# Strassen products for two more token pairs of K in layer two, later reloads, and four weight sums in front of an eviction

## The chip, the cores and the metric

The kernel runs on one core of a Trainium2 chip. A core has five engines, each with a queue of its own that it works off in order: TensorE (PE; its weight loads, PEld, overlap its matmuls), VectorE (DVE), ScalarE (ACT), GpSimd (POOL) and SyncE (SP), which here only issues DMAs. Matmuls write to PSUM, eight banks of 128 x 512 f32; everything else is in one large SBUF tensor, "arena". Engines wait for each other on semaphores. The metric is device time in microseconds, the median of several runs.

## The reference

Two blocks, A and B, are applied twice in turn to x, 2048 tokens of 1024 channels: A, B, A, B. "Layer one" is the first A and B, "layer two" the second.

```python
def _A_ref(x, wqkv, wo):               # H = 32 heads of Dh = 32
    q, k, v = split(x @ wqkv)
    phi = lambda t: jnp.where(t > 0, t + 1, jnp.exp(t)) + 1e-6
    pq, pk = phi(q), phi(k)
    kv = jnp.einsum("bhsd,bhse->bhde", pk, v)
    z = jnp.einsum("bhsd->bhd", pk)
    num = jnp.einsum("bhqd,bhde->bhqe", pq, kv)
    den = jnp.einsum("bhqd,bhd->bhq", pq, z)[..., None] + 1e-6
    return (num / den) @ wo
def _B_ref(x, w_gate, w_up, w_down):   # F = 3584
    return ((x @ w_gate) * (x @ w_up)) @ w_down
x = x + _A_ref(_layernorm(x), wqkv, wo)
x = x + _B_ref(_layernorm(x), w_gate, w_up, w_down)
```

(`split` stands for the reshape into q, k and v by heads.)

## The kernel before

**Strassen products.** Large products are cut into 2 x 2 blocks and done with seven block products instead of eight (one level), those of block B in part with a second level inside. The sums of operand blocks that this needs are made by VectorE (`tt`, line 849). The joins of partial results are VectorE additions from PSUM to PSUM with a copy that ScalarE made before.

**Order.** The program writes every engine's queue by hand. Each instruction goes in with the bytes and banks that it reads and writes, and the waits follow from that. So the order in which the Python code calls its steps is the order of every queue, SP's among them.

**K and Q of block A.** The 16 token tiles of 128 are taken as 8 pairs. K of a pair is either plain (line 979: four steps of eight 128x512 matmuls, two tiles by two halves of the columns, 32 in all) or by one Strassen level (line 1175: seven steps of four matmuls, 28 in all). In layer two all of Q (pairs 0 to 6 here) is by Strassen; K is plain for pairs below `KP0` and by Strassen from there on. The seven steps, in their order, use four PSUM banks A, B, C, D:

- step 0 multiplies into A, and ScalarE copies A to B (line 1187 for K, 1185 for Q);
- step 1 uses the sum s1, into C, and ScalarE copies C away (1191);
- step 2 uses s2, into B, and VectorE joins B and the copy into D (1179);
- step 3 finishes A;
- step 4 uses s3, into B, and a join into C follows (1179);
- step 5 uses s4 and finishes D;
- step 6 finishes B, which it must not touch before the join of step 4 has read it.

A finished bank goes through an exponential on ScalarE (1077, 1073) and on VectorE through a minimum (658 for K, 656 for Q; not where the exponential came with a bias) and an eviction (1104, or 1093 for two banks at once in plain pairs). GpSimd adds K to its running sum (1014).

A table of tokens, `KQ_SEQ`, sets the order of these steps. `K21` is step 1 of K of pair 2, `Q05` step 5 of Q of pair 0. `S20` to `S23` are the token sums s1 to s4 for pairs 2 and 3 together (line 849, 128x2x512), which K and Q share; `S40` and `S60` do the same for the pairs from 4 and 6. `L` moves the layer norm on by a step (ScalarE 474 and 494 for the statistics of a token tile, GpSimd 476, 496 and 498, VectorE 508, then a store to `xn_scratch` and a DMA transpose). `X` reloads one tile of normalized tokens from `xn_scratch`, `V`, `W` and `O` load weights. The last steps of a pair (its evictions) are issued one step of the table later.

**The end of block A's first stage.** The product of K and the normalized tokens (line 1409) comes next. Its first matmul needs all 16 reloaded tiles.

**Block B, the down pass.** Seven products, named by digits; the last, "3", is in layer one's first pass by a second level (`two_level`, lines 2044 to 2070): seven steps 1, 5, 6, 7, 2, 3, 4 for two parts p, with ScalarE copies (2048, 2062), VectorE joins (2051) and evictions (`evict`, 852). Between its steps the next pass is begun: `pro` is a list of that pass's first steps, and `pro_step(pro, 1)` calls them until one has put a matmul in. Among them are four weight sums (849, `sums`) that the next pass's first second-level product (1676) needs.

Of the kernel before, what the change touches and what calls it, by code (L numbers as in the profile page):

```python
# [180 lines left out]
def build_kernel(nc, A_x, A_wqkv, A_wo, B_w_gate, B_w_up, B_w_down, out):  # L181
# [14 lines left out]
    KSTR = True  # L196
    NEB = 3
    KQ_SEQ = {True: "L S30 Q20 S31 T L K30 S32 K31 L K32 Q21 S33 L Q22 K33 T S40 Q23 Q30 K40 K41 S41 L K42 Q31 Q32 Q33 L S42 K43 L Q34 K50 L Q35 Q36 S50 S43 K51 L Q40 L S51 S52 K52 Q41 Q42 Q43 L K53 Q44 Q45 L K60 Q46 K61 S60 Q50 S53 K62 Q51 S61 Q52 S62 Q53 Q54 K63 Q55 Q56 K70 Q60 K71 Q61 S63 Q62 L K72 Q63 Q64 Q65 K73 Q66 V",
              False: "K00 S00 S01 K01 S02 S03 L K02 K03 K10 L X K11 Q00 K12 Q01 X L Q02 K13 Q03 Q04 K20 X S20 Q05 S21 K21 S22 L Q06 S23 Q10 K22 X Q11 Q12 K23 Q13 L K30 X Q14 S40 Q15 S41 K31 S42 Q16 S43 Q20 X L K32 Q21 Q22 K33 Q23 X K40 Q24 L K41 Q25 K42 Q26 X K43 Q30 K44 K45 L Q31 K46 X Q32 Q33 K50 Q34 S60 K51 Q35 S61 L X S62 K52 S63 Q36 K53 Q40 K54 Q41 X K55 Q42 L K56 Q43 K60 Q44 K61 X Q45 K62 Q46 K63 L Q50 K64 X Q51 K65 Q52 K66 Q53 K70 L X Q54 K71 Q55 K72 Q56 K73 X Q60 K74 L Q61 K75 Q62 K76 Q63 X Q64 L Q65 Q66 V W O"}
    L1P0 = 3  # L200
    L1QS = 3
    QLAG = 0.409
# [3 lines left out]
    SPOS = 0.867  # L206
    SSTEP = 0.063
    CUP = 9
    KP0 = 4

    L2SETS = {(False, 0): "15", (False, 1): "15", (True, 0): "1532", (True, 1): "1532"}
    ORDERS = {
# [78 lines left out]
    P = _Prog(V_PT + 64)  # L291
# [42 lines left out]
    with ExitStack() as es:  # L334
# [1230 lines left out]
        def layer_B(lnp, nxt, first):  # L1565
# [322 lines left out]
            def down(ps_, ticks, tail, pro=()):  # L1888
# [26 lines left out]
                l2j = "3" if first and ps_ == 0 else ""  # L1915
# [90 lines left out]
                def two_level(q):  # L2006
# [47 lines left out]
                    for si, i in enumerate((1, 5, 6, 7, 2, 3, 4)):  # L2054
                        for p in range(2):
                            hi, lo = dst[p], dst[p + 2]
                            if i == 1:
                                mm(1, p, tmp[p], 0, True)
                                seed(p, hi)
                            elif i == 5:  # L2060
                                mm(5, p, tmp[p], 1, False)
                                P.add("act", (lambda p: lambda e: e.copy(c5[p][0], psb(tmp[p])[:, 256:512]))(p), prd=[tmp[p]], wr=c5[p][1])
                            elif i == 6:
                                mm(6, p, tmp[p], 0, False)
                                join(p, hi)
                            elif i == 2:
                                mm(2, p, hi, 0, False)
                            elif i == 3:
                                mm(3, p, hi, 1, False)
                                evict(p, hi)  # L2070
                            elif i == 7:
                                mm(7, p, tmp[p], 0, False)
                                seed(p, lo)
                                join(p, lo)
                            else:
                                mm(4, p, lo, 0, False)
                                evict(p + 2, lo)
                            if q == "3" and i in (3, 4):
                                pro_step(pro, 1)
                        if q != "3" and i in (1, 5, 7, 2):  # L2080
                            ex_pop(2 if l2j else 1)
                        if l2j and i == 1:
                            SQ.pop(0)()
                        if i in ((1, 3) if l2j else (5, 7, 3, 4)):
                            ring_issue()
                        if i in (5, 7, 3, 4):
                            ticks(q, {5: 0, 7: 1, 3: 2, 4: 3}[i])
# [26 lines left out]
                for qi, q in enumerate(DPROD[first, ps_]):  # L2114
# [13 lines left out]
                    for hf in range(2):  # L2128
                        n = n_of[q, str(hf)]
# [241 lines left out]
```

## Time and profile before

| | |
|---|---|
| median of 3 runs | 1433.35 us (1432.63 to 1433.55) |
| the profiled execution: time, span | 1432.78 us, 1431.0 us |
| instructions on TensorE, VectorE, ScalarE, GpSimd | 8430, 2024, 1540, 309 |
| K and Q stage of layer two | about 730.6 to 824.8 us of the span |
| end of layer one's first down pass | about 475.8 to 489.6 us |

In the rows that follow, times are us from the start of the span, and a row of the timeline has start, duration, engine, line, operation, output and inputs, and a count where equal instructions were merged. What stands in brackets is the engine's idle time ahead of it and what ended it. A row of groups has busy time and the mean duration in ns. SPq is SP's issuing of DMAs. A matmul of 512 columns shows 379 ns from its start to its end, though the next begins after 216.

### The profile page before, as it was taken

What the parts mean: (1) busy time and instruction counts of PE and PEld (TensorE: products, weight loads), DVE (VectorE), ACT (ScalarE), POOL (GpSimd) and SP (SyncE); (2) the same over time, 40 slices, a digit from 0 to 9 for tenths busy, and PEclk for the clock granted to TensorE, in tenths of its full rate; (3) what the DMA queues carried; (4) which work ended last, traced back from release to release, by engine and by line L of the source; (5) the groups of instructions that cost most, each with busy time, mean ns of one, the idle gap of its engine ahead of it and who ended that gap; (6) DMA issues with size and microseconds to landing.
All of it is one profiled execution on the core that took longest, in us unless ns stands there. A gap on an engine that the chain in (4) does not pass through costs nothing.

```text
span 1431.0 us, 22547 instructions
## 1 busy us (share of the span) xinstructions
PE 1421.5 (99%) x8430; PEld 813.3 (57%) x8430; DVE 1166.9 (82%) x2024; ACT 733.2 (51%) x1540; POOL 296.8 (21%) x309
## 2 busy tenths in 40 slices
PE   9999999999999999999999999999999999999999
PEld 4444444555544655554764444456666477666658
DVE  7878887889878799878878878779877877777886
ACT  4752367777720255552256523667776116777521
POOL 5644632000000000003334346301000400000160
PEclk9999999999999999999999999999999999999999
DMA  7316867987977999985798167589986689788657
GB/s 235 106 28 183 182 136 196 284 294 251 318 284 246 332 303 290 299 258 199 274 338 210 35 176 171 131 226 271 284 260 199 226 305 309 251 263 261 211 192 254
DMA packets 362541, 331.73 MB, mean 232 GB/s; under 512 B 178496, under 2 KB 305472, under 8 KB 361920
## 3 DMA queue, kind: packets, MB, share of 16 engines
q1 hardware_dynamic: 362432, 330.29, 76.9%
q8 instruction: 66, 1.08, 0.3%
q14 instruction: 43, 0.35, 0.1%
HBM read 239.27 MB, written 67.37 MB: 214 GB/s over the span
## 4 chain that ended last, share of the span: by engine, by line
PE 93%; DVE 3%; ACT 1%; DMA 1%; issue 1%; SPq 1%; POOL 1%; DVEq 0%; ACTq 0%
PE ps L1601 25%; PE ps L1676 17%; PE ps L2139 14%; PE ps L2044 9%; PE ps L1507 8%; PE ps L1409 8%; PE ps L1175 6%; PE ps L979 4%; PE ps L989 2%; DVE arena L849 1%; DMA arena<-in_B_w_down_dram 1%; PE ps L1421 1%; ACT arena L494 0%; DMA arena<-in_A_x_dram 0%; SPq L442 0%
## 5 line engine op out<-in xcount | busy, mean ns | idle before, releaser
L849 DVE TENSOR_TENSOR arena<-arena 128x512 f16<-128x512 f16 (+9 forms) x784 | 476.7, 636 | 73.0 <-ACT arena L1720 45.1
L1601 PE MATMUL ps<-arena 128*128 128x512 f16 x1808 | 446.8, 379 | 0.6 <-ACT ps L1631 0.6
L1676 PE MATMUL ps<-arena 128*128 128x256 f16 x2324 | 312.2, 273 | 2.1 <-DVE arena L849 0.9
L852 DVE SCALAR_TENSOR_TENSOR arena<-ps,arena 128x512 f16<-128x512 f32 (+2 forms) x396 | 263.0, 685 | 43.8 <-PE ps L2139 17.9
L1676 PEld LDWEIGHTS ps<-arena 128*128 128x128 f16 (+1 forms) x2324 | 226.1, 98 | 105.1 <-DVE ps L1695 4.7
L1601 PEld LDWEIGHTS ps<-arena 128*128 128x128 f16 (+1 forms) x1808 | 176.6, 98 | 141.7 <-ACT ps L1631 1.1
L2139 PE MATMUL ps<-arena 128*128 128x512 f16 (+1 forms) x896 | 194.2, 379 | 0.0
L1606 ACT ACTIVATE arena<-ps 128x512 f16<-128x512 f32 x224 | 134.1, 598 | 91.7 <-PE ps L1601 89.7
L2092 POOL TENSOR_TENSOR arena<-arena 128x512 f32<-128x512 f32 x44 | 69.8, 1596 | 424.5 <-ACT arena L2090 339.5
L2139 PEld LDWEIGHTS ps<-arena 128*128 128x128 f16 x896 | 87.7, 98 | 105.7
L2044 PE MATMUL ps<-arena 128*128 128x256 f16 (+1 forms) x1176 | 130.3, 273 | 0.1
L2044 PEld LDWEIGHTS ps<-arena 128*128 128x128 f16 x1176 | 114.5, 98 | 15.2 <-DVE ps L2051 0.4
L1695 DVE TENSOR_TENSOR ps<-ps,arena 128x256 f32<-128x256 f32 x220 | 92.3, 428 | 31.9 <-PE ps L1676 16.3
L1409 PE MATMUL ps<-arena 128*128 128x512 bf16 x512 | 115.4, 379 | 0.0
L485 POOL TENSOR_SCALAR arena<-arena 128x1 f32<-128x1 f32 x43 | 16.4, 382 | 472.5 <-DVE arena L484 472.5
L1507 PE MATMUL ps<-arena 128*128 128x512 bf16 x512 | 111.5, 379 | 0.0
L1692 ACT COPY ps<-ps 128x256 f32<-128x256 f32 x220 | 81.1, 368 | 51.4 <-PE ps L1676 43.8
L1175 PE MATMUL ps<-arena 128*128 128x512 bf16 (+1 forms) x420 | 95.1, 379 | 0.4 <-DVE ps L1179 0.3
L1315 POOL TENSOR_TENSOR arena<-arena 128x1024 f16<-128x1024 f32 x32 | 79.8, 2494 | 69.6 <-DVE arena L1313 61.7
L1631 ACT COPY ps<-ps 128x512 f32<-128x512 f32 x112 | 64.2, 573 | 49.2 <-PE ps L1676 43.5
L1014 POOL TENSOR_TENSOR arena<-arena 128x512 f32<-128x512 f32 x60 | 73.6, 1245 | 69.4 <-DVE arena L1104 33.6
L1507 PEld LDWEIGHTS ps<-arena 128*128 128x128 f16 x512 | 50.1, 98 | 59.8
(81 smaller groups left out, 1275.8 us busy)
## 6 DMA issues: line engine op xcount, KB each, us to landing
arena<-w_scratch SPq DMA_DIRECT2D x84, 512.0 KB, 5.1
arena<-sp_scratch SPq DMA_DIRECT2D x56, 512.0 KB, 5.8
arena<-t_scratch SPq DMA_DIRECT2D x27, 896.0 KB, 5.9
arena<-in_B_w_down_dram SPq DMA_DIRECT2D x18, 896.0 KB, 7.0
w_scratch<-arena SPq DMA_DIRECT2D x28, 512.0 KB, 5.9
sp_scratch<-arena SPq DMA_DIRECT2D x28, 512.0 KB, 4.1
arena<-in_B_w_gate_dram SPq DMA_DIRECT2D x42, 256.0 KB, 5.2
arena<-in_B_w_up_dram SPq DMA_DIRECT2D x42, 256.0 KB, 3.6
```

What stands on the lines that cost most here:

```text
L849: P.add("dve", lambda e: e.tensor_tensor(out=out, in0=a, in1=b, op=op), rd=rd, wr=wr, prd=prd)
L852: P.add("dve", lambda e: e.scalar_tensor_tensor(out=out, in0=a, scalar=sc, in1=b, op0=ALU.mult, op1=op1), rd=rd, wr=wr, prd=prd)
L1175: P.add("pe", lambda e: [e.matmul(psb(bank), x[:, k, :], w[:, k, :], start=(start and k == 0), stop=(k == 3), skip_group_check=True) for k ...
L1409: return [e.matmul(psb(bank), xr[:, t, j * 128:(j + 1) * 128], pk[:, h, t, :], start=(t == 0), stop=(t == NST - 1)) for t in range(NST)]
L1507: return [e.matmul(psb(bank), xnT[:, g, i * 128:(i + 1) * 128], wp[:, g, dh * 512:(dh + 1) * 512], start=(dh == 0 and g == 0), stop=(g == ...
L1601: P.add("pe", lambda e: [e.matmul(psb(bank), w[:, k, :], x[:, k, :], start=(start and k == 0), stop=(k == 3), skip_group_check=True) for k ...
L1606: P.add("act", lambda e: e.activation(t, psb(bank), AF.Copy, scale=SG), prd=[bank], wr=r)
L1676: P.add("pe", lambda e: [e.matmul(psb(bank)[:, 256 * half:256 * half + 256], w[:, k, :], xx[:, k, :], start=(start and k == 0), stop=(k == ...
L1692: P.add("act", lambda e: e.copy(psb(dst[c])[:, 0:256], lo), prd=[bk], pwr=[dst[c]])
L1695: P.add("dve", lambda e: e.tensor_tensor(out=psb(dst[c])[:, 256:512], in0=lo, in1=c5, op=ALU.add), prd=[bk], rd=rc5, pwr=[dst[c]])
L2044: P.add("pe", lambda e: [e.matmul(psb(bank)[:, 256 * half:256 * half + 256], a[:, k, :], w[:, k, :], start=(start and k == 0), stop=(k == ...
L2139: return [e.matmul(psb(bank), hv[:, 7 * hf + k, t * 128:(t + 1) * 128], w[:, k, :], start=(start and hf == 0 and k == 0), stop=(hf == 1 an ...
```

## The change

`KP0` goes from 4 to 2: K of pairs 2 and 3 of layer two is by Strassen too, so six pairs in all. The table's order for layer two is new; among other things the first reload of normalized tokens comes after K of pair 3 instead of early in pair 1. And in `two_level`, in layer one's first pass, the next pass's steps are called behind step 2 of the second part until one has put a VectorE instruction in.

```diff
-              False: "K00 S00 S01 K01 S02 S03 L K02 K03 K10 L X K11 Q00 K12 Q01 X L Q02 K13 Q03 Q04 K20 X S20 Q05 S21 K21 S22 L Q06 S23 Q10 K22 X Q11 Q12 K23 Q13 L K30 X Q14 S40 Q15 S41 K31 S42 Q16 S43 Q20 X L K32 Q21 Q22 K33 Q23 X K40 Q24 L K41 Q25 K42 Q26 X K43 Q30 K44 K45 L Q31 K46 X Q32 Q33 K50 Q34 S60 K51 Q35 S61 L X S62 K52 S63 Q36 K53 Q40 K54 Q41 X K55 Q42 L K56 Q43 K60 Q44 K61 X Q45 K62 Q46 K63 L Q50 K64 X Q51 K65 Q52 K66 Q53 K70 L X Q54 K71 Q55 K72 Q56 K73 X Q60 K74 L Q61 K75 Q62 K76 Q63 X Q64 L Q65 Q66 V W O"}
+              False: "K00 S00 S01 K01 S02 S03 L K02 K03 K10 L K11 Q00 K12 Q01 L Q02 K13 Q03 Q04 K20 S20 Q05 S21 K21 S22 L Q06 S23 K22 Q10 K23 Q11 K24 L K25 Q12 K26 Q13 K30 Q14 K31 L Q15 K32 Q16 S40 K33 S41 Q20 S42 K34 L S43 K35 Q21 K36 X Q22 Q23 K40 Q24 L K41 Q25 X K42 Q26 K43 Q30 K44 L X K45 Q31 K46 Q32 X Q33 K50 Q34 L S60 K51 Q35 S61 X K52 Q36 S62 K53 Q40 S63 L K54 X K55 Q41 K56 Q42 X Q43 K60 Q44 L K61 Q45 X K62 Q46 K63 X Q50 K64 X K65 Q51 X K66 Q52 X Q53 K70 L Q54 X K71 Q55 K72 X Q56 K73 X Q60 K74 L X K75 Q61 K76 Q62 Q63 Q64 Q65 Q66 V W O"}
...
-    KP0 = 4
+    KP0 = 2
...
                             elif i == 2:
                                 mm(2, p, hi, 0, False)
+                                if l2j and p:
+                                    n = len(P.streams["dve"])
+                                    while len(P.streams["dve"]) == n:
+                                        pro.pop(0)()
```

TensorE, where K of pair 2 begins, before: Q04, K20 in plain form (L979), Q05 (it waits for a weight block, d_qb3), K21, and Q06 (d_ptq3 is another). A name s_... is an engine's semaphore, d_... that of a DMA.

```order
L1175 MATMUL ps<-arena 128x512 [waits s_dve]
L1175 MATMUL ps<-arena 128x512 x3
L979 MATMUL ps<-arena 128x512 x8
L1175 MATMUL ps<-arena 128x512 [waits d_qb3]
L1175 MATMUL ps<-arena 128x512 x3
L979 MATMUL ps<-arena 128x512 x8
L1175 MATMUL ps<-arena 128x512 [waits d_ptq3,s_dve]
L1175 MATMUL ps<-arena 128x512 x3
```

The same place after the change: Q04 and K20, Q05 (d_qb3), K21 (d_ptk0 is a weight block of K), Q06, then K22, Q10, K23 and Q11.

```order
L1175 MATMUL ps<-arena 128x512 [waits s_dve]
L1175 MATMUL ps<-arena 128x512 x7
L1175 MATMUL ps<-arena 128x512 [waits d_qb3]
L1175 MATMUL ps<-arena 128x512 x3
L1175 MATMUL ps<-arena 128x512 [waits d_ptk0,s_dve]
L1175 MATMUL ps<-arena 128x512 x3
L1175 MATMUL ps<-arena 128x512 [waits d_ptq3]
L1175 MATMUL ps<-arena 128x512 x3
L1175 MATMUL ps<-arena 128x512 [waits s_act,s_dve]
```

K20 and K21 have four matmuls each instead of eight, and K21 waits for VectorE, whose sum S20 it reads.

VectorE at the same place before the change, from the join of Q04 (L1179) on. The four L849 rows are S20 to S23; L658 with L1093 is the first tile of K of pair 2.

```order
L1179 TENSOR_TENSOR ps<-ps,arena 128x512 [waits s_pe]
L656 TENSOR_SCALAR arena<-arena 128x512 [waits s_act]
L1104 SCALAR_TENSOR_TENSOR arena<-ps,arena 128x512 [waits s_dve]
L1104 SCALAR_TENSOR_TENSOR arena<-ps,arena 128x512 [waits s_act]
L849 TENSOR_TENSOR arena<-arena 128x2x512
L849 TENSOR_TENSOR arena<-arena 128x2x512 [waits s_dve]
L1104 SCALAR_TENSOR_TENSOR arena<-ps,arena 128x512 [waits s_act]
L849 TENSOR_TENSOR arena<-arena 128x2x512
L508 TENSOR_SCALAR arena<-arena 128x1024 [waits d_ns12,d_tl0,s_pool]
L658 TENSOR_SCALAR arena<-arena 128x1024 [waits s_act]
L1093 SCALAR_TENSOR_TENSOR arena<-ps,arena 128x2x512 [waits s_dve]
L849 TENSOR_TENSOR arena<-arena 128x2x512
```

And after the change, from the same L508 (the layer norm's step) on, which is where the two queues part:

```order
L508 TENSOR_SCALAR arena<-arena 128x1024 [waits d_ns12,d_tl0,s_pool]
L849 TENSOR_TENSOR arena<-arena 128x2x512 [waits s_dve]
L1179 TENSOR_TENSOR ps<-ps,arena 128x512 [waits s_act,s_pe]
L1104 SCALAR_TENSOR_TENSOR arena<-ps,arena 128x512 [waits s_act]
L658 TENSOR_SCALAR arena<-arena 128x512 [waits s_act]
L1104 SCALAR_TENSOR_TENSOR arena<-ps,arena 128x512 [waits s_dve]
L1179 TENSOR_TENSOR ps<-ps,arena 128x512 [waits s_pe]
```

Up to that L508 the queue is the same. Then S23 moves ahead of K's evictions, two joins of K22 and K24 (L1179) are new, and K's evictions are single ones (L1104 of 128x512).

VectorE at the end of layer one's first down pass: the four joins of product "3", its evictions (L852) and the four weight sums (L849; d_rr4 and d_rr3 are the loads of the weights).

```order
 L2051 TENSOR_TENSOR ps<-ps,arena 128x256 [waits s_act] x2
-L852 SCALAR_TENSOR_TENSOR arena<-ps,arena 128x512 [waits s_pe]
 L849 TENSOR_TENSOR arena<-arena 128x512 [waits d_ds1,d_rr4]
 L849 TENSOR_TENSOR arena<-arena 128x512 [waits d_rr3,s_dve]
 L849 TENSOR_TENSOR arena<-arena 128x512
 L849 TENSOR_TENSOR arena<-arena 128x512 [waits s_dve]
-L852 SCALAR_TENSOR_TENSOR arena<-ps,arena 128x512 [waits s_pe]
+L852 SCALAR_TENSOR_TENSOR arena<-ps,arena 128x512 [waits s_pe] x2
```

The first eviction, which waits for TensorE, now stands behind the sums instead of ahead of them. On SP, the reloads `arena<-xn_scratch` leave their places between the stores and transposes of the layer norm: one of them stays ahead of the last transpose and fifteen follow behind it.

## The prediction

> **What bounds the kernel now.** First the page: totals and the chain of work that ended last.
>
> ```profile
> span 1431.0 us, 22547 instructions
> PE 1421.5 (99%) x8430; PEld 813.3 (57%) x8430; DVE 1166.9 (82%) x2024; ACT 733.2 (51%) x1540; POOL 296.8 (21%) x309
> PE 93%; DVE 3%; ACT 1%; DMA 1%; issue 1%; SPq 1%; POOL 1%; DVEq 0%; ACTq 0%
> ```
>
> TensorE carries the chain. So an edit pays what it takes off TensorE's queue, or the idle time that it opens or closes there. Next, the chain by place: the K and Q stage of layer two, and the last product ("3") of layer one's first down pass.
>
> ```profile
> 771.16 1.73 PE ps L979 x8
> 772.89 51.91 PE ps L1175 x240
> 824.79 6.91 PE ps L1409 x32
> ```
>
> The 240 Strassen matmuls follow each other at 51.91/240 = 0.216 us, without a gap, and the next stage follows at once. A group of four takes 0.865 us and a plain group of eight 1.73 us.
>
> ```profile
> 475.78 8.42 PE ps L2044 x77
> ...
> 484.83 0.43 DVE arena L849
> 485.26 0.05 issue
> 485.31 0.39 PE ps L1676 x2
> ```
>
> Here the chain leaves TensorE: two matmuls of L1676 wait for the first weight sum (L849).
>
> **Part 1, the four sums in front of an eviction.** The timeline around it, and the load that feeds the sums:
>
> ```profile
> 474.30 0.38 SPq L442 DMA_DIRECT2D arena<-in_B_w_up_dram  x1
> 482.32 0.43 DVE L2051 TENSOR_TENSOR ps<-ps,arena 128x256 f32<-128x256 f32 x1 [0.33 <-ACT ps L2048]
> 484.03 0.38 PE L1676 MATMUL ps<-arena 128*128 128x256 f16 x2
> 484.23 0.69 DVE L852 SCALAR_TENSOR_TENSOR arena<-ps,arena 128x512 bf16<-128x512 f32 x1 [1.47 <-PE ps L2044]
> 484.83 1.55 DVE L849 TENSOR_TENSOR arena<-arena 128x512 f16<-128x512 bf16 x4
> DMA to landing us min/median/max: 2.9/5.5/7.5
> ```
>
> VectorE sits idle from 482.75 to 484.23, waiting to evict, and the sums stand behind. Moved ahead, they run from 482.8 to 484.35; the first ends at 483.2, before TensorE asks for it at 484.25. Their load was issued at 474.30 and with the longest landing of that stretch, 7.5 us, is there at 481.8. The eviction is late by 484.35 - 484.23 = 0.1 us, and what reads its bank comes later. The second pair of matmuls starts at 484.25 instead of 485.31: a gain of 1.06 us. Behind it, TensorE's next short waits (on the copy and the join of the same product) shift along with it. The gain lies between 0 (the load is late after all) and 1.2; I take 1.06.
>
> **Part 2, K of pairs 2 and 3 by Strassen.** Each pair has 28 matmuls instead of 32: 8 fewer, 8 x 0.216 = 1.73 us off TensorE. VectorE and ScalarE get more, priced by these rows of the stretch in question and of the steady stretch behind it:
>
> ```profile
> L1093 DVE SCALAR_TENSOR_TENSOR arena<-ps,arena 128x1024 bf16<-128x1024 f32 x5 | 6.1, 1225 | 0.2
> L1104 DVE SCALAR_TENSOR_TENSOR arena<-ps,arena 128x512 bf16<-128x512 f32 x9 | 6.1, 687 | 0.3 <-ACT arena L1073 0.2
> L1179 DVE TENSOR_TENSOR ps<-ps,arena 128x512 f32<-128x512 f32 x4 | 2.8, 691 | 0.2 <-PE ps L1175 0.2
> L658 DVE TENSOR_SCALAR arena<-arena 128x1024 bf16<-128x1024 bf16 x5 | 2.1, 427 | 4.5 <-ACT arena L1077 4.5
> 782.92 0.29 DVE L658 TENSOR_SCALAR arena<-arena 128x512 bf16<-128x512 bf16 x1 [0.67 <-ACT arena L1077]
> L1191 ACT COPY arena<-ps 128x512 f32<-128x512 f32 x2 | 1.2, 590 | 0.1
> L1187 ACT COPY ps<-ps 128x512 f32<-128x512 f32 x1 | 0.6, 570 | 0.9 <-DVE arena L1093 0.9
> core 0: us, PE busy (x) PEld busy (x) DVE busy (x) ACT busy (x) POOL busy (x), PEclk, DMA share, GB/s
> 748.00:776.00 28.00, 28.00 (x132) 12.50 (x131) 24.69 (x37) 18.25 (x32) 14.88 (x18) 1.00 0.89 192
> ```
>
> A plain pair costs VectorE two minima of 1024 and two double evictions, 2 x (0.43 + 1.23) = 3.3 us; a Strassen pair four small minima, four evictions and two joins, 4 x (0.29 + 0.69) + 2 x 0.69 = 5.3 us. Two pairs: +4.0 us where the stretch had 28.00 - 24.69 = 3.3 us of slack, and that shrinks by the 1.73 us. ScalarE gets two copies more a pair, +2.3 us. So VectorE has no cover left there, and its order decides. The first wait can be read straight off the trace, because up to the sum S20 nothing on VectorE's queue changes:
>
> ```profile
> 747.86 0.44 DVE L658 TENSOR_SCALAR arena<-arena 128x1024 bf16<-128x1024 bf16 x1 [1.86 <-ACT arena L1077]
> 748.34 1.22 DVE L1093 SCALAR_TENSOR_TENSOR arena<-ps,arena 128x1024 bf16<-128x1024 f32 x1
> 749.48 0.69 DVE L1179 TENSOR_TENSOR ps<-ps,arena 128x512 f32<-128x512 f32 x1
> 750.07 0.87 DVE L656 TENSOR_SCALAR arena<-arena 128x512 bf16<-128x512 bf16 x1
> 750.98 1.29 DVE L1104 SCALAR_TENSOR_TENSOR arena<-ps,arena 128x512 bf16<-128x512 f32 x2
> 752.19 0.68 DVE L849 TENSOR_TENSOR arena<-arena 128x1024 f16<-128x1024 f16 x1
> 748.55 1.89 PE L979 MATMUL ps<-arena 128*128 128x512 bf16 x8
> 750.28 1.03 PE L1175 MATMUL ps<-arena 128*128 128x512 bf16 x4
> ```
>
> S20 is the row at 752.19; it ends at 752.87. Until now only Q of pair 2 read it, much later. After the change K21 reads it, two groups of four behind K13: K20 from 748.55, Q05 from 749.42, K21 due at 750.28. It can start at 752.92: TensorE idle for 2.64 us, more than the 1.73 us saved. Between 0 (a sum that is early) and 2.64 I take the upper end, since both times are rows of the trace and what stands ahead is the same.
>
> From there I add up by hand, in the new order: VectorE's evictions and joins follow each other at 0.60 (two in 1.29), ScalarE's exponentials at 0.55, and one token's normalization holds ScalarE for 2.33 (744.92 to 747.25 below).
>
> ```profile
> 744.92 1.15 ACT L494 ACTIVATE arena<-arena 128x1024 bf16<-128x1024 bf16 x1
> 746.19 1.06 ACT L474 ACTIVATE arena<-arena 128x1024 bf16<-128x1024 bf16 x1
> 747.25 1.24 ACT L1077 ACTIVATE arena<-ps 128x512 bf16<-128x512 f32 x2
> ```
>
> K21 ends at 753.95, K24 at 759.1, K26 at 761.7, K30 at 763.5. ScalarE does K24's exponential at 760.25, then a token's normalization until 763.1, and K26's exponential only at 763.7. Its eviction ends at 765.7, the copy that opens pair 3 (its bank) at 766.3, so K32 is late by 0.45 us. Q16 then waits 0.3 us for a join. ScalarE's lag holds VectorE: the join of K32 starts at 769.3, and before the join of K34 come three evictions with one minimum and the sums S40, S41, S42. That join ends at 775.15 on VectorE; K36, which must wait for it (it writes the bank that the join reads), would be due at 772.74: 2.46 us. Q24 loses 0.07. In pair 5, K56 now stands two groups behind K54 instead of three; the join of K54 would end 0.4 us after K56 is due. Sum of waits 2.64 + 0.45 + 0.3 + 2.46 + 0.07 + 0.4 = 6.3 us. The first is read, the others rest on a chain of additions; their bounds are 0 and, with the joins a further sum (0.68) late each, about 6.
>
> **Part 3, the reloads of normalized tokens.** Most of the sixteen loads go from the stretch with a DMA share of 0.89 into one that has room, and on SP they no longer stand ahead of the transposes of later tokens. No wait of VectorE on a transpose shows before, so I put the gain at 0, bounds 0 and 0.3. They were spread from pair 1 on and now go out behind the last transpose, near 780:
>
> ```profile
> 776.00:825.00 49.00, 49.00 (x228) 22.04 (x227) 42.62 (x75) 28.69 (x50) 19.40 (x18) 1.00 0.31 90
> 778.75 1.24 SPq L593 DMA_TRANSPOSE arena<-arena  x1
> 780.04 5.02 SPq L442 DMA_DIRECT2D arena<-xn_scratch  x8
> ```
>
> Eight issues took 5.02 us, so fifteen take 9.4 and are out by about 793, 30 us ahead of their first reader at 824.79. Cost 0; it would show only if SP were held some 25 us.
>
> **Sum.** The profiled execution took 1432.78 us for its span of 1431.0. It becomes 1432.78 - 1.73 - 1.06 + 6.3 = 1436.3. The median of the runs, 1433.35, is 0.57 above that execution, so I expect a median of 1436.9, +0.25%. The runs spread by 0.06%; I call 0.2%, 2.9 us, what a measurement can tell from no change.
>
> **Rivals.**
> - Not slower: only K21's wait stands. ScalarE and VectorE empty their queues during the 2.64 us, and the join of K34 is done by 772.7. Then -1.73 - 1.06 + 2.64 = -0.15 us, 1433.2. For it: TensorE's idle time is time in which both catch up. Against it: the lag that I found comes from normalizations that run later. It decides when that join runs 2.4 us earlier than I add up.
> - Faster side: S20 gets done in time and no wait opens; -2.8 us, 1430.6, which is -0.19%. It needs VectorE to reach S20 by 749.6, and the trace has it busy through 752.19.
> - The first wait lets the clock fall. TensorE's first ten matmuls show the price:
>
> ```profile
> 1.36 4.11 PE L449 MATMUL ps<-arena 128*128 128x512 f16 x10 [1.36 <-POOL arena L445]
> ```
>
>   They took 4.11 us where ten at 0.216, with 0.16 for the last to end, take 2.3: 1.8 us an episode. Behind two such waits that is 3.6 us more, 1440.5. Against it: the granted clock is 1.00 in both windows quoted, though neither has a pause of 2.6 us.
>   The Trainium skill, "TensorE: Matmul & The Clock Gate", Part 1, speaks against this change here: it says that the clock halves once the array has been idle over a whole window, which it puts at about 3.4 us. By that rule a wait of 2.64 us would not fill a window, and the sum stays at 1436.9; only waits that join would bring 1440.5. No row before the change shows such a pause, so the trace neither agrees nor disagrees.
> - The gain of part 1 is lost (the load lands late): +1.06, 1438.0 with the rest as forecast, within the forecast's own range below.
>
> **Chances.** Forecast, waits of 4.5 to 8 us: 0.50. Only the first wait, or little more: 0.30. No wait: 0.09. The clock: 0.04. Longer waits, up to 1440: 0.07. The forecast's own range, 1435.1 to 1438.6, lies for some seven tenths beyond the 0.2% line at 1436.2, which with the last two cases gives slower 0.47; no wait passes -0.2% in about half of its cases, with reloads that help, so faster 0.05; the rest, 0.48, is within 0.2%. The range 1431.5 to 1440.0 leaves out most of "no wait" and the top of the last two.
>
> **What would show it.** Right: in the waits of the changed kernel, TensorE or its weight load at L1175 waits for VectorE's L849 once, for about 2.6 us near 750.3 less the 1.06 us, and again for L1179 near K36; L1175 has 476 matmuls and L979 288; the wait of L1676 near 485 is gone. Wrong: S20 starts earlier than 751.1 in the new trace, or K36 finds its join done. A granted clock below 1.00 behind K21 would mean the third rival.

## The result and the profile after

The changed kernel takes 1438.76 us (median of six runs, 1437.14 to 1439.90) against 1432.93 us of the kernel before on the same chip (1432.52 to 1433.55): 1.0042 times, 95% interval 1.0032 to 1.0052, or 5.8 us slower. The forecast was 1436.9. The profiled execution took 1439.9 us. Its totals, and the engines on the chain that ended last:

```profile
span 1438.2 us, 22546 instructions
PE 1423.0 (99%) x8422; PEld 813.8 (57%) x8422; DVE 1167.7 (81%) x2036; ACT 734.4 (51%) x1544; POOL 295.8 (21%) x309
PE 94%; DVE 2%; ACT 2%; issue 1%; DMA 0%; SPq 0%; POOL 0%; DVEq 0%; ACTq 0%
```

TensorE has its 8 matmuls less and is still busy 1.5 us longer; the totals alone don't say why. First the end of layer one's first down pass, in the chain:

```profile
476.91 8.41 PE ps L2044 x77
485.32 0.44 PE ps L1676 x4
485.76 0.76 PE ps L2044 x7
...
489.02 0.66 PE ps L1676 x6
489.67 1.73 PE ps L1601 x8
```

Four matmuls of L1676 now follow at once, and VectorE's L849 has left the chain. In the timeline, from the first L2044 of the last part to the first L1601 it is 13.84 us before and 12.76 after. This execution came to 476.91 late by 1.13 us (before: 475.78). Near the start of the program a wait of TensorE at L599 took 2.5 us instead of 0.7, and TensorE's granted clock, the third number from the end in these rows, then fell (before, it is 1.00 in both windows):

```profile
core 0: us, PE busy (x) PEld busy (x) DVE busy (x) ACT busy (x) POOL busy (x), PEclk, DMA share, GB/s
0.00:10.00 10.00, 5.87 (x21) 2.39 (x22) 4.03 (x8) 2.36 (x3) 4.20 (x24) 0.89 0.80 248
10.00:30.00 20.00, 19.76 (x112) 9.77 (x111) 16.11 (x30) 8.76 (x14) 9.92 (x14) 0.97 0.86 296
```

Both lie far ahead of the two edits, and e3, which has the edits too, comes to its K and Q stage 1.84 us earlier (728.64), so this late start is not put down to the change. The 1.08 us won in the down pass hide it: at 489.67 both kernels are level. All that is lost lies in the K and Q stage, in TensorE's timeline:

```profile
746.88 3.62 PE L1175 MATMUL ps<-arena 128*128 128x512 bf16 x16
752.97 13.12 PE L1175 MATMUL ps<-arena 128*128 128x512 f16 x60 [2.48 <-DVE arena L849]
767.13 6.48 PE L1175 MATMUL ps<-arena 128*128 128x512 f16 x28 [1.03 <-ACT ps L1187]
775.83 26.03 PE L1175 MATMUL ps<-arena 128*128 128x512 f16 x112 [2.22 <-DVE ps L1179]
802.19 29.77 PE L1175 MATMUL ps<-arena 128*128 128x512 f16 x136 [0.33 <-DVE ps L1179]
831.80 0.38 PE L1409 MATMUL ps<-arena 128*128 128x512 bf16 x1
```

Each row is a run of matmuls up to the next pause of note, and the bracket is that pause. The stage, from its first L979 (730.48; before 730.42) to the first L1409 (before 824.63), takes 101.32 us instead of 94.21, 7.1 more. At 0.2162 us a matmul, each row says by how much the next one starts late: K21 (752.97) 2.63, K32 (767.13) 1.19, K36 (775.83) 2.65, of which 0.27 is a small pause inside the row ahead (at Q16), K56 (802.19) 2.15, and L1409 0.21, small pauses inside the last row. K56's is mostly no wait at all: 112 matmuls took 26.03 us where 24.4 would do. The stretches there, again with the granted clock as the third number from the end:

```profile
767.00:776.00 9.00, 6.56 (x29) 2.69 (x30) 7.78 (x14) 4.76 (x10) 4.11 (x5) 0.99 0.24 58
776.00:778.00 2.00, 2.00 (x6) 0.69 (x5) 1.97 (x5) 1.63 (x4) 0.17 (x1) 0.50 0.35 128
778.00:780.00 2.00, 2.00 (x8) 0.82 (x7) 1.44 (x3) 0.33 (x1) 1.01 (x1) 0.68 0.97 245
780.00:785.00 5.00, 5.00 (x25) 2.25 (x23) 3.67 (x8) 2.92 (x5) 2.41 (x3) 1.00 1.00 333
```

Behind K36's pause TensorE ran at half its clock: 1.00 us lost in the second row, 0.64 in the third and 0.09 in the first, 1.73 in all, or about 3.4 us at 0.50. (The 26.03 us are 1.66 too many; the first row's 0.09 is a rounded figure.) Behind K21's pause, which was longer, the clock stayed at 1.00.

### The profile page after: what moved, and what is told of

The parts are those of the page before. It is cut to its first block, busy times and chain, and to the rows that moved or that the text cites. A ratio compares the mean times of both kernels' runs of the same rounds, so it can differ in the third digit from the quotient of the medians.

```text
span 1438.2 us, 22546 instructions
## 1 busy us (share of the span) xinstructions
PE 1423.0 (99%) x8422; PEld 813.8 (57%) x8422; DVE 1167.7 (81%) x2036; ACT 734.4 (51%) x1544; POOL 295.8 (21%) x309
## 3 DMA queue, kind: packets, MB, share of 16 engines
q8 instruction: 66, 1.08, 0.3%
## 4 chain that ended last, share of the span: by engine, by line
PE 94%; DVE 2%; ACT 2%; issue 1%; DMA 0%; SPq 0%; POOL 0%; DVEq 0%; ACTq 0%
PE ps L1601 27%; PE ps L1676 18%; PE ps L2143 13%; PE ps L2044 9%; PE ps L1507 8%; PE ps L1409 8%; PE ps L1175 5%; PE ps L979 4%; PE ps L989 3%; DVE arena L849 1%; ACT arena L494 1%; DVE arena L1104 1%; PE ps L1421 1%; PE ps L1449 0%; DVE ps L1179 0%
## 5 line engine op out<-in xcount | busy, mean ns | idle before, releaser
L849 DVE TENSOR_TENSOR arena<-arena 128x512 f16<-128x512 f16 (+9 forms) x784 | 474.5, 633 | 72.8 <-ACT arena L1720 45.1
L1601 PE MATMUL ps<-arena 128*128 128x512 f16 x1808 | 446.9, 379 | 0.6 <-ACT ps L1631 0.6
L1676 PE MATMUL ps<-arena 128*128 128x256 f16 x2324 | 312.0, 273 | 0.7 <-ACT arena L1720 0.6
L852 DVE SCALAR_TENSOR_TENSOR arena<-ps,arena 128x512 f16<-128x512 f32 (+2 forms) x396 | 263.0, 686 | 43.5 <-PE ps L2143 17.9
L1676 PEld LDWEIGHTS ps<-arena 128*128 128x128 f16 (+1 forms) x2324 | 226.3, 98 | 103.2 <-DVE ps L1695 3.5
L1601 PEld LDWEIGHTS ps<-arena 128*128 128x128 f16 (+1 forms) x1808 | 176.6, 98 | 141.7 <-ACT ps L1631 1.1
L2143 PE MATMUL ps<-arena 128*128 128x512 f16 (+1 forms) x896 | 194.2, 379 | 0.0
L2044 PE MATMUL ps<-arena 128*128 128x256 f16 (+1 forms) x1176 | 130.3, 273 | 0.1
L2044 PEld LDWEIGHTS ps<-arena 128*128 128x128 f16 x1176 | 114.5, 98 | 15.2 <-DVE ps L2051 0.4
L1409 PE MATMUL ps<-arena 128*128 128x512 bf16 x512 | 115.4, 379 | 0.0
L1175 PE MATMUL ps<-arena 128*128 128x512 f16 (+1 forms) x476 | 108.6, 384 | 6.5 <-DVE ps L1179 2.9
```

Source lines behind the costliest of these rows:

```text
L849: P.add("dve", lambda e: e.tensor_tensor(out=out, in0=a, in1=b, op=op), rd=rd, wr=wr, prd=prd)
L852: P.add("dve", lambda e: e.scalar_tensor_tensor(out=out, in0=a, scalar=sc, in1=b, op0=ALU.mult, op1=op1), rd=rd, wr=wr, prd=prd)
L1175: P.add("pe", lambda e: [e.matmul(psb(bank), x[:, k, :], w[:, k, :], start=(start and k == 0), stop=(k == 3), skip_group_check=True) for k ...
L1409: return [e.matmul(psb(bank), xr[:, t, j * 128:(j + 1) * 128], pk[:, h, t, :], start=(t == 0), stop=(t == NST - 1)) for t in range(NST)]
L1601: P.add("pe", lambda e: [e.matmul(psb(bank), w[:, k, :], x[:, k, :], start=(start and k == 0), stop=(k == 3), skip_group_check=True) for k ...
L1676: P.add("pe", lambda e: [e.matmul(psb(bank)[:, 256 * half:256 * half + 256], w[:, k, :], xx[:, k, :], start=(start and k == 0), stop=(k == ...
```

## The experiments

The theory: TensorE waits because VectorE, whose work grows with one-level pairs, comes late to single instructions (a sum, a join), and the clock falls behind some of these waits. The rivals: the reloads' new places cost something; the waits come from the order alone and can be ordered away; the sums are not what makes VectorE late. The table has, for each kernel, its median and that of the kernel before measured with it, the ratio with its interval, and from its profile the length of the K and Q stage, the waits of L1175 by the profile (longest in brackets), and how many executions had a mean granted clock under 1.000.

| kernel | us | before | ratio | stage, us | waits, us | clock < 1.000 |
|---|---|---|---|---|---|---|
| after | 1438.76 | 1432.93 | 1.0042 [1.0032, 1.0052] | 101.32 | 6.4 (2.5) | 4 of 6 |
| e1 four weight sums alone | 1431.87 | 1432.64 | 0.9995 [0.9986, 1.0004] | 94.21 | 0.3 (0.3) | 1 of 11 |
| e2 K and the table alone | 1440.78 | 1432.64 | 1.0057 [1.0043, 1.0070] | 102.59 | 6.1 (2.5) | 3 of 4 |
| e3 reloads where they were | 1439.09 | 1432.64 | 1.0046 [1.0032, 1.0060] | 99.93 | 6.4 (2.5) | 3 of 4 |
| e4 S20 to S23 early | 1436.51 | 1432.64 | 1.0025 [1.0015, 1.0035] | 97.81 | 4.4 (2.2) | 5 of 8 |
| e5 S40 to S43 late | 1440.61 | 1432.06 | 1.0057 [1.0045, 1.0070] | 101.18 | 7.8 (2.5) | 4 of 5 |
| e6 both | 1437.70 | 1432.06 | 1.0038 [1.0025, 1.0051] | 99.84 | 5.1 (2.5) | 4 of 5 |
| e7 and S60 to S63 late | 1437.52 | 1432.06 | 1.0037 [1.0024, 1.0049] | 99.59 | 6.1 (2.5) | 0 of 5 |
| e8 and a layer-norm step later | 1437.31 | 1432.06 | 1.0034 [1.0022, 1.0046] | 98.62 | 5.2 (2.5) | 2 of 6 |
| e9 one sum behind each join | 1435.12 | 1432.47 | 1.0019 [1.0010, 1.0028] | 97.99 | 4.5 (1.5) | 0 of 11 |
| e10 and the layer-norm steps spread | 1433.56 | 1432.47 | 1.0009 [1.0001, 1.0018] | 96.25 | 3.0 (0.7) | 2 of 11 |
| e11 with short sums | 1430.77 | 1432.84 | 0.9988 [0.9979, 0.9997] | 93.60 | 0.6 (0.3) | 1 of 11 |
| e12 with sums on GpSimd | 1433.96 | 1432.84 | 1.0009 [1.0001, 1.0018] | 97.01 | 3.6 (1.0) | 4 of 11 |

A stage contains any clock fall that its execution had, so compare medians too. The waits are those of the whole profile; 0.3 us of each lie in layer one, as in the kernel before. The last column counts falls anywhere in the program, and some have nothing to do with this stage: of 71 executions of the kernel before in these sessions 6 are under 1.000, and in the profiled executions of e8 and e12 the only fall lies in the first 12 us, behind short waits of 1.3 and 0.5 us. The contrast is large all the same: the kernels with a pause of over 2 us in the stage (after, e2 to e8) have 25 of 43, the others (e1, e9 to e12) 8 of 55.

### The parts by themselves: e1, e2, e3

e1 is the kernel before with only this:

```diff
                                 mm(2, p, hi, 0, False)
+                                if l2j and p:
+                                    n = len(P.streams["dve"])
+                                    while len(P.streams["dve"]) == n:
+                                        pro.pop(0)()
```

> The kernel before with the four weight sums in front of the eviction, and nothing else of the change. If the wait of L1676 for L849 near 485 us was the whole cost there, the time falls by 1.06 us against before (1431.9). The rival, that the stretch behind it is held by its loads (DMA share 0.99), gives the gain back by 652 us and the time stays where it was.

e2 is the kernel after without these four lines.

> The changed kernel without the four sums in front: K of pairs 2 and 3 by Strassen with the new table. If the two parts are independent, the time is that of the changed kernel plus 1.1 us (about 1439.8), so 6.9 us over before, with TensorE idle at K21 for 2.5 us, at K32 for 1.0 and at K36 for 2.2. If the sums shift what happens in K and Q, the difference is another.

e3 is the kernel after with the sixteen reloads at the places of before; the first rows of the table's difference:

```diff
-K03 K10 L K11 Q00 K12 Q01 L Q02 K13 Q03 Q04 K20 S20 Q05
+K03 K10 X L K11 Q00 K12 Q01 X L Q02 K13 Q03 Q04 K20 X S20 Q05
...
-K35 Q21 K36 X Q22 Q23 K40 Q24 L K41 Q25 X K42
+K35 Q21 K36 Q22 Q23 X K40 Q24 L K41 Q25 K42
```

> The changed kernel with the reloads of normalized tokens back behind the same steps as in the kernel before (from pair 1 on). If they move nothing on the path, as I hold, the time equals that of the changed kernel (1438.8, within 0.5). The rival: the moved reloads had relieved the transposes and the sums, and the time rises by some us; or they were what the K part suffers from, and it falls towards 1433.

Measured: e1 has no wait of L1676 for L849 any more, the same 12.76 us at that place as after, and the K and Q stage of before. Its median is 0.77 us lower than before's, with an interval (-2.0 to +0.6 us) that holds both the 1.06 us and no change. The gain is shown by the traces (13.84 against 12.76 us, in each of the twelve kernels that have the sums in front 12.76 or 12.77), not by the times. e2 keeps all the loss; its median is 2.0 us above that of after where 1.1 were expected, and its profiled execution had two clock falls in the stage. TensorE's timeline of e2, the rows from K21 on and from K36 on:

```profile
753.73 14.81 PE L1175 MATMUL ps<-arena 128*128 128x512 f16 x60 [2.48 <-DVE arena L849]
...
777.95 25.94 PE L1175 MATMUL ps<-arena 128*128 128x512 f16 x112 [2.22 <-DVE ps L1179]
```

and the same rows of e3:

```profile
751.13 13.12 PE L1175 MATMUL ps<-arena 128*128 128x512 f16 x60 [2.47 <-DVE arena L849]
...
773.99 24.64 PE L1175 MATMUL ps<-arena 128*128 128x512 f16 x112 [2.22 <-DVE ps L1179]
```

The same two pauses to 0.01 us; in e2's execution both runs of matmuls behind them are long (14.81 and 25.94 us), in e3's neither (13.12 and 24.64), in that of after only the second. So a pause of 2.2 to 2.5 us is followed by a fall of the clock in some executions and not in others. The reloads' places change nothing that shows: the stage of e3 is shorter than that of after by 26.03 - 24.64 = 1.39 us, which is the fall alone (1.66 us, less a pause of 0.28 us ahead of Q24 that e3 has and the slowed TensorE of after has not), and the medians agree.

### The two waits by name: e4, e5, e6, e7

e4 takes the sums of pairs 2 and 3 out of K21's way, everything else as after:

```diff
-K03 K10 L K11 Q00 K12 Q01 L Q02 K13 Q03 Q04 K20 S20 Q05 S21 K21 S22 L Q06 S23 K22
+K03 S20 K10 S21 L K11 Q00 K12 S22 Q01 L Q02 S23 K13 Q03 Q04 K20 Q05 K21 L Q06 K22
```

> The changed kernel with the sums S20 to S23 issued between the steps of K of pairs 0 and 1, where VectorE waited before. My theory: the wait at K21 (2.6 us) is gone; what stands behind it loses the head start that the wait gave to VectorE and ScalarE, so the waits at K32 and K36 may stay or grow. Between 1434 (both shrink) and 1438.8 (the wait only moves to K36). If the wait at K21 were not due to the place of S20 on VectorE's queue, it would stay.

K21's wait is gone, K32's grows from 1.0 to 1.5 us, the others stay, and the median falls by 2.25 us. The intervals of the two ratios overlap a little, but the stages without a clock fall, 97.81 us against 99.93 in e3, say the same. This part of the theory stands. e5 does the same for K36, whose join (of K34) had S40, S41 and S42 ahead of it on VectorE:

```diff
-K32 Q16 S40 K33 S41 Q20 S42 K34 L S43 K35 Q21 K36 X Q22 Q23
+K32 Q16 K33 Q20 K34 L K35 S40 Q21 S41 K36 S42 X Q22 S43 Q23
```

> The sums of pairs 4 and 5 (S40 to S43) are moved from ahead of K35 to between K35 and Q23, the rest as in the kernel after. Theory (the join of K34 is late because three sums stand in front of it on VectorE): the wait of K36 for L1179 falls from 2.22 us to under 0.5 us, K21's wait for L849 (2.5 us) and K32's for L1187 (1.0 us) stay. From the 1436.67 us of the execution whose clock stayed at 1.00 (reloads put back), that is 1434.2 to 1434.6 us; with a clock fall of 1.7 us behind K21 in some executions, up to 1436.3, so a median of 1434.2 to 1436. Rival (something else is late there anyway, an exponential or a copy on ScalarE): K36's wait stays at 1.5 us or more under another name, and the median stays at 1437.5 or above.

e6 has both edits, e7 also that of the next sums (`K54 S60 X K55 S61 Q41 K56 S62 Q42 S63`).

> S20 to S23 as in the run in which they were early, S40 to S43 as in the run in which they were late: both waits of over 2 us are taken away. Theory one (the clock falls only behind waits of 2 us and more): the granted clock is 1.00 in every execution, the times lie within 1.5 us of each other, and the profiled time is 1436.67 - 2.5 - 2.2 + 0.45 (K32's wait, 1.47 instead of 1.03) = 1432.4 us; range of the median 1431.8 to 1433. Theory two (the falls come with the one-level products themselves, whatever the waits): executions with a clock of 0.998 or 0.999 are still among them, and the median is 1433 to 1434.5.

> As the run before it, with the sums of pairs 6 and 7 (S60 to S63) moved from ahead of K53 to behind K54 to Q42. Theory (three of them stand ahead of the join that K56 waits for): K56's wait of 0.33 us goes, 0.3 to 0.5 us less than the run before, median 1431.5 to 1432.7. Rival (the sums only move the wait to a later place in the Q products): no difference, or a new wait in Q42 to Q44.

All three missed. e5 is no faster than after, e6 lies 5 us above its expectation, and the wait is still there under another name. TensorE and VectorE in e6's timeline:

```profile
771.03 3.63 PE L1175 MATMUL ps<-arena 128*128 128x512 f16 x16 [0.41 <-DVE ps L1179]
777.16 22.58 PE L1175 MATMUL ps<-arena 128*128 128x512 f16 x94 [2.50 <-DVE ps L1179]
...
772.72 0.68 DVE L849 TENSOR_TENSOR arena<-arena 128x1024 f16<-128x1024 f16 x1
773.32 0.29 DVE L658 TENSOR_SCALAR arena<-arena 128x512 bf16<-128x512 bf16 x1
773.64 0.69 DVE L1104 SCALAR_TENSOR_TENSOR arena<-ps,arena 128x512 bf16<-128x512 f32 x1
774.25 2.24 DVE L849 TENSOR_TENSOR arena<-arena 128x1024 f16<-128x1024 f16 x2
776.41 0.69 DVE L1179 TENSOR_TENSOR ps<-ps,arena 128x512 f32<-128x512 f32 x1
```

K36 (771.03) waits 0.41 us instead of 2.2: that join is cured. But the three sums now stand ahead of the next join, that of Q22 (776.41), and Q24, which writes the bank it reads, waits 2.50 us. (Two of them took 2.24 us together, where two run in 1.4 when GpSimd is not adding.) In e7, too, K56's wait only changed places (0.28, and 0.74 a little later). What e6 was to tell of the clock it could not tell, since a pause of over 2 us was still there.

### Order or amount: e8 to e12

e8 moves one layer-norm step, which on ScalarE stood in front of K26's exponentials, out of e7's way:

```diff
-K24 L K25 Q12 K26 Q13 K30 Q14
+K24 K25 Q12 K26 Q13 K30 L Q14
```

> As the run before it, with the layer-norm step behind K24 moved to behind K30, so that on ScalarE its two passes (1.15 and 1.06 us) no longer stand in front of K26's exponentials. Theory (K32's wait for the copy L1187 comes from these passes): the wait of 1.0 to 1.5 us falls under 0.3 us, the 240 - 8 matmuls of the stage run without a gap of over 0.4 us, and the time is 1.2 to 1.5 us less than the run before: median 1430.0 to 1431.3, 1.5 to 2.5 us below the kernel before. Rival (the copy waits for VectorE's eviction, whose minima and fused evictions take turns with GpSimd's sums, whatever ScalarE does): the wait stays at 1 us or more.

The wait for the copy L1187 is gone from its list of waits and K32 starts on time, as expected; the joins, 4.6 us in e7, took part of it back:

```profile
PE ps L1175 <- DVE ps L1179: 5.2, 8, 2.5
```

(total, times, longest). The stage is 0.97 us shorter than that of e7, the median 0.21. So the next question was whether an order is to blame at all. e9 is e4 with the eight sums of pairs 4 to 7 behind eight different joins, so that no two of them stand ahead of the same one.

```diff
-K32 Q16 S40 K33 S41 Q20 S42 K34 L S43 K35 Q21 K36 X Q22 Q23 K40 Q24 L
+K32 S40 Q16 K33 Q20 K34 S41 L K35 Q21 K36 X Q22 S42 Q23 K40 Q24 S43 L
...
-Q34 L S60 K51 Q35 S61 X K52 Q36 S62 K53 Q40 S63 L K54 X K55 Q41 K56 Q42 X
+Q34 L K51 Q35 X K52 S60 Q36 K53 Q40 L K54 S61 X K55 Q41 K56 Q42 S62 X
```

(S63 goes behind K62.)

> S20 to S23 early; of S40 to S43 and S60 to S63 each stands alone behind another join (S40 behind K32, S41 behind K34, S42 behind Q22, S43 behind Q24; S60 behind K52, S61 behind K54, S62 behind Q42, S63 behind K62). Theory (a join has about one sum's time, 0.6 us, to spare, and three sums ahead of one join cost TensorE 2.2 to 2.5 us wherever the group stands): no wait for L1179 is over 0.7 us, all of them together under 1.5 us; K32's wait for the copy L1187 stays at 1.0 to 1.5 us; 1434.96 - 2.2 = 1432.8 us, range of the median 1432 to 1433.8. Rival (VectorE has too much work for the whole stretch from 765 to 800 us, however it is ordered): the waits for L1179 add up to 2.5 us or more, in smaller pieces, and the median stays above 1434.5.

e10 adds to it the layer-norm steps from K24 to Q44, now behind K30, Q21, K43, Q31, Q33, Q34, K55 and Q44.

> As the run before it, and the eight layer-norm steps from K24 to Q44 are moved to other gaps between two joins, so that none stands in front of K26's exponentials or shares a gap of three groups with a sum. Theory: K32's wait goes to under 0.4 us besides, all waits of L1175 together stay under 2 us, and the time is 1430.5 to 1432, no slower than the kernel before with the four weight sums alone (1431.87). Rival (VectorE has too much work for the stretch): the waits only move, the median is within 1 us of the run before it.

The waits of L1175 in e9's profile:

```profile
PE ps L1175 <- DVE ps L1179: 3.0, 5, 1.0
PE ps L1175 <- ACT ps L1187: 1.5, 1, 1.5
```

and in e10's:

```profile
PE ps L1175 <- DVE ps L1179: 3.0, 6, 0.7
```

No wait for a join is over 1.0 us (the theory said 0.7), but together they are 3.0 us, as the rival said; e4 had 2.9 with three sums in one heap, and before has 0.3. The stage of e9 (97.99) is no shorter than that of e4 (97.81). Spreading the sums saved none of VectorE's lateness. What it did save is the clock: none of e9's 11 executions is under 1.000, against 5 of 8 of e4, and its median is 1.4 us lower (though the intervals of the two ratios overlap). The three executions of e4 that are at 1.000 have a median of 1435.10, so without a fall the two kernels are equal. e10 is another 1.56 us lower, K32's wait, as expected; the waits for joins stay at 3.0 us, which was not, and the kernel is 1.0009 times the one before. That leaves whether the sums are at fault at all. e11 is e10 with the sums of pairs 4 to 7 formed over 16 of 128 columns.

```diff
-                        tt(o4[:, PL[o - 1]], v[0], v[1], f, rd, rs(o))
+                        tt(*[y[..., :16 if m == 2 and p >= 4 else 128] for y in (o4[:, PL[o - 1]], *v)], f, rd, rs(o))
```

> The run before it, with the eight sums of pairs 4 to 7 formed over 16 of their 128 columns only: most of these sums is left out of the computation, the order is the same. Theory (VectorE's time for the sums is what the joins are late by): each sum falls from 0.6 to about 0.15 us, the waits for L1179 after pair 3's copy fall from 3.0 to under 1.2 us together, and the time by 1.8 to 3 us, to 1430.6 to 1431.8. Rival (the joins are late for the chain of exponentials, minima and evictions of the one-level pairs themselves, sums or none): the waits stay at 2 us or more and the time falls by less than 1 us.

e12 has these sums whole, but on GpSimd:

```diff
-                        tt(o4[:, PL[o - 1]], v[0], v[1], f, rd, rs(o))
+                        P.add("pool" if m == 2 and p >= 4 else "dve", lambda e: e.tensor_tensor(out=o4[:, PL[o - 1]], in0=v[0], in1=v[1], op=f), rd=rd, wr=rs(o))
```

> As the run with one sum behind each join and moved layer-norm steps, with the eight sums of pairs 4 to 7 on GpSimd instead of VectorE. If VectorE's time for the sums is the cause, the waits for L1179 fall to about 1 to 1.5 us and the time to 1431 to 1432.3. Rival: a sum takes GpSimd about 2.3 us (twice the 1.15 us of its 128x512 add), VectorE's minima are slow beside it (0.28 becomes 1.06 us as beside the adds L1014), eight times some 0.8 us; then the waits stay at 3 us or grow, and the products of pair 4 may wait for a sum: 1433.5 to 1437.

VectorE's groups in e10 from 728 to 826 us (busy us, mean ns of one):

```profile
L849 DVE TENSOR_TENSOR arena<-arena 128x1024 f16<-128x1024 f16 x16 | 12.3, 778 | 0.0
L658 DVE TENSOR_SCALAR arena<-arena 128x512 bf16<-128x512 bf16 x24 | 9.3, 388 | 3.1 <-ACT arena L1077 3.0
...
L656 DVE TENSOR_SCALAR arena<-arena 128x512 bf16<-128x512 bf16 x7 | 5.3, 763 | 0.0
```

the same in e11:

```profile
L658 DVE TENSOR_SCALAR arena<-arena 128x512 bf16<-128x512 bf16 x24 | 8.9, 371 | 3.4 <-ACT arena L1077 3.0
L849 DVE TENSOR_TENSOR arena<-arena 128x1024 f16<-128x1024 f16 x8 | 5.7, 729 | 0.0
...
L849 DVE TENSOR_TENSOR arena<-arena 128x128 f16<-128x128 f16 x8 | 3.5, 435 | 0.0
L656 DVE TENSOR_SCALAR arena<-arena 128x512 bf16<-128x512 bf16 x7 | 3.4, 489 | 0.0
```

and e11's one line of waits at L1175:

```profile
PE ps L1175 <- DVE ps L1179: 0.6, 2, 0.3
```

A short sum takes 0.435 us in the mean, three times what I had expected. That mean hides two kinds: five sums took 0.21 or 0.22 us, and the three that ran beside an addition of GpSimd 0.63 to 0.97. From e11's timeline:

```profile
767.31 1.16 POOL L1014 TENSOR_TENSOR arena<-arena 128x512 f32<-128x512 f32 x1 [3.35 <-DVE arena L1104]
767.74 0.81 DVE L849 TENSOR_TENSOR arena<-arena 128x128 f16<-128x128 f16 x1
788.52 0.22 DVE L849 TENSOR_TENSOR arena<-arena 128x128 f16<-128x128 f16 x1
```

The sums gave VectorE 12.3 - 5.7 - 3.5 = 3.1 us back. The minima, as many as before, took 2.3 us less besides (L658 0.4, L656 1.9). TensorE's stage shrank by 96.25 - 93.60 = 2.65 us, and the median by 2.8; the waits for joins are nearly gone, and the stage is now 0.6 us shorter than that of before. So it is VectorE's time that the joins are late by, and three different orders left them late by much the same. How much of that time is the sums' own, and how much is lost beside GpSimd's additions, stays open: no run takes those additions away. e12 shows that GpSimd is no way out. Its waits (L1153 is where the sums are now issued), two of VectorE's groups, the minima and the sums that stayed, and two of GpSimd's sums in the timeline:

```profile
PE ps L1175 <- DVE ps L1179: 2.2, 4, 1.0
PE ps L1175 <- POOL arena L1153: 1.4, 2, 0.7
```

```profile
L658 DVE TENSOR_SCALAR arena<-arena 128x512 bf16<-128x512 bf16 x24 | 13.6, 565 | 4.5 <-ACT arena L1077 4.4
...
L1153 DVE TENSOR_TENSOR arena<-arena 128x1024 f16<-128x1024 f16 x8 | 5.7, 729 | 0.0
```

```profile
764.51 4.43 POOL L1153 TENSOR_TENSOR arena<-arena 128x1024 f16<-128x1024 f16 x2
```

A sum takes 2.2 us there. VectorE is rid of 12.3 - 5.7 = 6.6 us of sums, but its minima beside GpSimd take 13.6 us instead of 9.3, so 4.3 us are lost again, and two products wait for a sum directly. No version with six pairs that forms its sums whole beat the kernel before (e11 leaves most of eight of them out); the best whole kernel tried is e1, whose lead is within its interval.

## Why the prediction was right, and where it was not

Slower, because VectorE comes late to K21's sum and to the joins, was forecast and is what happened; the median lies 1.9 us above the forecast.

**Part 1.** Forecast -1.06 us, measured -1.08 at its place. The load was in time and nothing behind gave the gain back. The rival that this gain is lost falls.

**Part 3.** Forecast 0, measured none (e3).

**Part 2, the first wait.** K21: forecast 2.64, measured 2.63 us. It could be read off the old trace, because nothing ahead of S20 on VectorE had changed.

**Part 2, the waits added up by hand.** Forecast K32 0.45, Q16 0.3, K36 2.46, Q24 0.07, K56 0.4; measured in e3, whose clock stayed at 1.00, 1.18, 0.26, 2.38, 0.28 and 0.48. With K21 they come to 7.2 us, inside the 4.5 to 8 us of the forecast's case. K36 is right although both of its ends came 0.6 to 0.7 us later in after than I had added up (due at 773.45, join done at 775.77): the same lateness moved both. The step "K26's exponential only at 763.7. Its eviction ends at 765.7" mis-sized K32. Timeline of after:

```profile
763.71 1.06 DVE L658 TENSOR_SCALAR arena<-arena 128x512 bf16<-128x512 bf16 x1 [1.16 <-ACT arena L1077]
...
763.46 1.15 POOL L1014 TENSOR_TENSOR arena<-arena 128x512 f32<-128x512 f32 x1
```

The minimum that I took at 0.29 us took 1.06 beside GpSimd's addition, 0.77 more, and K32 is 0.74 later than forecast. The Trainium skill, "Advanced Engine Details and Errata", section VectorE Performance Modes, says that GpSimd shares VectorE's second SBUF port and that VectorE's two-port modes and GpSimd block each other; this row and e12's minima (565 ns instead of 388) agree.

**The clock.** The sum left it out, and the third rival, which had it, got a chance of 0.04 and a price of 1.8 us an episode. The price was right (1.73); its row shows a slow clock by the spacing of the ten matmuls, 0.43 us, though the granted clock reads 1.00 there. The chance was the error. It rested on the pause being too short. A fall was in the profiled execution of after, and four of its six executions have a mean clock under 1.000. By the prediction's own sign, a clock below 1.00 behind K21, the rival did not occur in this profile; the fall came behind K36. In e2's profile it came behind both. The fall, K32's 0.74 and the late start account for the miss of the profiled execution: against the forecast of 1436.3 for a profiled execution the measured 1439.9 has 1.7 us of clock, 0.74 of K32 and 1.1 of the late start, some 3.6 us in all, and the smaller terms nearly cancel. For the median, 1.9 us above the forecast, only mean clocks are on record: 0.998 twice (the profiled execution, with its two falls, is one of them), 0.999 twice, 1.000 twice. K32's 0.74 and a fall in some executions fit that size, but how many of these falls lie in the K and Q stage is not known.

**The rival that only K21's wait stands** (chance 0.30) falls: VectorE and ScalarE did not catch up during that pause, K36 still waited 2.2 us. Even without K21's pause (e4) it is the same 2.2.

**"Its order decides".** This half of a sentence of part 2 is half right, and no number of the forecast hung on it. Order decided K21's 2.5 us and K32's 1.0 to 1.5: e4 and e10 took them away. It did not decide the waits for joins. For these the sentence ahead had the reason: 4.0 us more for VectorE where 3.3 us, less the 1.73 us by which the stretch shrinks, were free, an overload of 2.4 us. The waits for joins in this stage are 2.6 to 2.7 us in e4, e9 and e10, three different orders, and e11 takes them away by taking work away. That the two sizes agree so well is in part luck, since the overload was priced for undisturbed instructions and for a shorter stretch.

## What to carry to other kernels

Where a cheaper product moves work to an engine that is already busy through the stretch, subtract its new work from its free time over the whole stretch first: here what did not fit came back on the bounding engine, and after the two waits that an order could cure, a new order only decided which instruction waited. Price that engine's work by where it will run: an addition that took VectorE 0.21 us by itself took 0.97 beside GpSimd. Count one long wait and many small ones as different things, too: a single pause of over 2 us could be followed by another 1.7 us of lost clock, pauses of at most 1.5 us in the same stage were not. When a wait is moved away and the time stays, look for the same microseconds at the next join on that queue.

## What the hardware showed

The granted clock fell to 0.50 behind pauses of TensorE of only 2.2 to 2.5 us, for about 3.4 us, in some executions and not in others. Of the twelve such pauses at L1175 in the profiles of after and of e2 to e8, four were followed by a fall (one in after, two in e2, one in e6); behind the pauses of 1.5 us and less in this stage none was. Near the start of the program, where TensorE's work is still broken up by short waits, it was otherwise: after's 2.5 us at L599 was followed by a fall, and in e8 and e12 one came behind 1.3 us at L599 and 0.5 us at L989, with 0.6 us of matmuls between them. In e6 the fall came about 1 us after TensorE had resumed:

```profile
771.00:777.00 6.00, 3.63 (x16) 1.49 (x16) 5.93 (x9) 2.66 (x5) 2.12 (x2) 1.00 0.74 198
777.00:779.00 2.00, 1.84 (x7) 0.81 (x8) 1.97 (x5) 0.57 (x1) 0.91 (x1) 0.75 1.03 377
779.00:781.00 2.00, 2.00 (x6) 0.66 (x5) 1.97 (x3) 0.00 (x0) 1.78 (x2) 0.50 1.02 384
781.00:783.00 2.00, 2.00 (x10) 0.88 (x9) 1.25 (x3) 1.75 (x3) 0.00 (x0) 0.89 1.05 405
```

The Trainium skill, "TensorE: Matmul & The Clock Gate", Part 1, gives a free-running window of about 3.4 us and half the clock after an idle one. The length of the falls and their chance nature agree with such a window; that a whole one must be idle does not, since no pause named here was longer than 2.5 us. What share of a window decides was not tried and stays open. So does why e7, with the same pause of 2.50 us as e6, shows 1.000 in all five executions.

GpSimd's 128x1024 f16 addition took 2.2 us where VectorE's takes 0.7, and slowed VectorE's minima as shown. A 128x128 f16 addition on VectorE took 0.21 us by itself and up to 0.97 beside one of GpSimd's 128x512 f32 additions; the three slowed ones all ended within 0.1 us of the end of GpSimd's.
